# Scale maxima, masks, loads, stores and order changed in a fused attention and mixture-of-experts kernel

## The chip, the cores and the metric

The kernel runs on one core of a Trainium2 chip. Its engines work from lists of their own: TensorE (PE; PEld is its loading of weights), VectorE (DVE), ScalarE (ACT), GpSimd (POOL), and SyncE (SP), which here issues the transfers. The metric is the device time of one execution in microseconds (us), lower is better.

## The reference, cut to what matters

```python
scores = scale * np.matmul(q, k.transpose(0, 1, 3, 2))      # q, k, v: (4, 8, 576, 64)
rel = pos[:, None] - pos[None, :]
scores = np.where((rel >= 0) & (rel < 64), scores, -1000000000.0)
attn = np.exp(scores - np.max(scores, axis=-1, keepdims=True))
attn = attn / (np.sum(attn, axis=-1, keepdims=True) + 1e-09)
x = np.matmul(attn, v)                      # then reshaped to (2304, 512)

h = x @ w_in                                # 512 -> 2048
g = h * np.tanh(np.log1p(np.exp(h)))        # for h > 20: h * tanh(h)
x2 = g @ w_out                              # 2048 -> 512

logits = x2 @ phi                           # 32 slots
d = softmax(logits, axis=0); c = softmax(logits, axis=1)
slot_input = d.T @ x2                       # 8 experts with 4 slots each
slot_out[e] = np.maximum(slot_input[e] @ w1[e], 0.0) @ w2[e]
out = c @ slot_out                          # (2304, 512)
```

## The kernel before, in words

The 2304 tokens are 18 tiles of 128. Three stages run into each other.

Attention: a tile has two blocks of 64 queries, and each block sees 128 keys, its own 64 and the 64 before. `t_qk` puts the mask (a bf16 matrix of 0 and a large negative number, `cb`) into PSUM by four matmuls (L361) and adds the scores to it (L370). VectorE takes the maximum of each row (`t_max`, L379), ScalarE or VectorE turns it into a bias (`t_neg`, L384, L386), and ScalarE makes the exponentials from PSUM (`t_exp`, L392), for tile 0 with their sums, which VectorE forms for the others (`t_sum`, L398). GpSimd normalizes (`t_norm`, L406), TensorE transposes (`a_tr`, L427), ScalarE copies back (`t_trev`, L432), TensorE multiplies with the values (`t_pv`, px, L440), and ScalarE or VectorE copies x (`t_x`, L448). Since the two blocks of a tile overlap in their keys, keys come in 12 and values in 18 loads of 512 KB, with each value in two of them.

First feed-forward: h = x @ w_in. Every float32 operand is split into a high and a low half-precision part (`xh` L619, `xl` L622; `wh` L503, L505, `wl`), scaled by powers of two, and three products of the parts are summed (`u_mm`, L629: 864 matmuls of 512 columns, called H here). The scales come from bounds on the maxima: TensorE multiplies the top halves of values (`v_gram`) and of w_in (`w_abs`) with themselves (`g_gram`, L416), and VectorE takes the largest entry of the diagonal. The large matrices arrive as 64-bit words and are decoded by ScalarE (L312) and two VectorE passes (L317, L321). ScalarE applies the activation (u, L635), with a table load where the function changes. g is split again: first half on GpSimd (`u_gh`, L649) or VectorE (L653), second on VectorE (`u_gl`, L656). It is transposed by transfers. g @ w_out is not computed for the tokens: logits are g @ (w_out @ phi), and A (L817) sums the rows of g weighted with the exponentials of the logits, over ten blocks of up to two tiles, by steps lr, lt (L762), e, et (L795), A.

Tail: w_out is applied to A, then the experts (`eh` L951, relu, `ho` L967 which moves the relu's output to the rows, `eo` L982), repetition of the outputs (`or`, L996), products with the combine weights (`fo`, L1022), copies (`ob`, L1026) and stores (L1035, L1037). The combine weights are a softmax over the 32 logits of a token (`c_max` to `c_mul`), transposed (`ct`, L1067) into a buffer.

The order is made by a planner (`Plan`) at build time. It holds every step with its engine, an assumed cost, a due time and what it needs, and pools of buffers: 53 slabs of 4 KB a partition, 8 PSUM banks, and limits on some kinds. It runs through time, and on each free engine emits the ready step with the least due time; `PRM` is the table of numbers behind the due times. Where TensorE has nothing ready in the front and in the tail it emits pads (`fill`, L230), products of zeros. `reserve` keeps slabs from the early loading of the experts' 64 weight parts of 512 KB.

## Time and profile before

| | us |
|---|---|
| median of three runs | 396.62 (395.6 to 396.87) |
| the profiled execution | 396.48 |
| its span | 394.70 |

| engine | busy us | share of the span | instructions |
|---|---|---|---|
| PE | 373.4 | 95% | 4359 |
| PEld | 219.2 | 56% | 4359 |
| DVE | 250.3 | 63% | 542 |
| ACT | 257.8 | 65% | 479 |
| POOL | 84.0 | 21% | 71 |

Transfers moved 102.72 MB. Along the chain of waits that ended last, PE holds 52% of the span, ACT 20%, DVE 8%, DMA 8% and issue 7%. A share of busy time is a mean over stages: the stretches have to be looked at one by one. Pads count as busy. A record on DVE or ACT may reach into the next one, so the time that an instruction adds to a full list is a little less than its record.

### The profile page before, as it was taken

How to read it: one execution, taken by the hardware profiler on the slowest of the kernel's cores; microseconds unless marked ns; L12 is line 12 of the kernel's file. 1: busy time of each engine (PE TensorE's matmuls, PEld its weight loads, DVE VectorE, ACT ScalarE, POOL GpSimd, SP SyncE). 2: the span in 40 equal slices, each digit the busy share in tenths (PEclk: the TensorE clock that was granted, in tenths of full speed). 3: DMA queues.
4: the chain of work that ended last, by engine and by line, in shares of the span. 5: the costliest groups of instructions: out<-in, count | busy, mean ns of one | idle time of the engine just before them, and what ended most of it. 6: DMA issues, size and time to landing. Idle time of an engine off the chain costs nothing.

```text
span 394.7 us, 10510 instructions
## 1 busy us (share of the span) xinstructions
PE 373.4 (95%) x4359; PEld 219.2 (56%) x4359; DVE 250.3 (63%) x542; ACT 257.8 (65%) x479; POOL 84.0 (21%) x71
## 2 busy tenths in 40 slices
PE   7999999999999999998999998999999999999870
PEld 6686766655566655754555444454444476437750
DVE  3689899979979994779785556433332677010350
ACT  4589988999999996685889999455271361000140
POOL 0054522042864524014131212212200000000000
PEclk9999999999999999999999999999999999999995
DMA  7999997606999937778899989999999679999387
GB/s 290 406 409 392 410 406 284 215 2 152 235 272 307 302 125 173 109 96 228 160 252 282 240 227 218 236 263 273 304 270 277 133 213 390 409 408 408 152 274 207
DMA packets 103071, 102.72 MB, mean 260 GB/s; under 512 B 78704, under 2 KB 83696, under 8 KB 103024
## 3 DMA queue, kind: packets, MB, share of 16 engines
q1 hardware_dynamic: 103024, 102.06, 87.6%
q8 instruction: 34, 0.56, 0.6%
q14 instruction: 13, 0.11, 0.1%
HBM read 79.50 MB, written 4.72 MB: 213 GB/s over the span
## 4 chain that ended last, share of the span: by engine, by line
PE 52%; ACT 20%; DVE 8%; DMA 8%; issue 7%; POOL 2%; SPq 0%; DVEq 0%; POOLq 0%; ACTq 0%
PE h L629 23%; ACT L635 4%; PE eo L982 4%; DMA gT<-gg 4%; ACT p L392 4%; PE eh L951 4%; ACT u L635 3%; PE pad L230 3%; ACT L312 3%; DMA v<-in_vL 2%; PE px L440 2%; PE pt L427 2%; PE A L817 2%; PE fo L1022 2%; DMA wir<-in_w_in 2%
## 5 line engine op out<-in xcount | busy, mean ns | idle before, releaser
L629 PE MATMUL h<-wh,xx 128*128 128x512 f16 x576 | 182.5, 379 | 0.0
L629 PEld LDWEIGHTS <-xx 128*128 128x128 f16 x864 | 80.7, 97 | 89.1 <-issue 2.3
L629 PE MATMUL h<-wl,xx 128*128 128x512 f16 x288 | 109.1, 379 | 0.0
L635 ACT ACTIVATE u<-h,sc 128x512 f32<-128x512 f32 x72 | 48.1, 686 | 49.5 <-PE h L629 46.8
L406 POOL TENSOR_TENSOR p<-p,st 128x512 f32<-128x512 f32 x36 | 44.7, 1260 | 91.9 <-DVE st L402 39.7
L656 DVE SCALAR_TENSOR_TENSOR gg<-u,sc,gg 128x1024 f16<-128x1024 f32 (+1 forms) x38 | 47.5, 1253 | 25.3 <-POOL gg L649 25.1
L649 POOL TENSOR_SCALAR gg<-u,sc 128x1024 f16<-128x1024 f32 x30 | 38.4, 1285 | 110.3 <-ACT u L635 104.7
L635 ACT ACT_TABLE_LOAD x35 | 44.9, 1283 | 0.7
L392 ACT ACTIVATE p<-s,st 128x128 f32<-128x128 f32 x144 | 42.6, 403 | 0.3
L398 DVE TENSOR_REDUCE st<-p 128x4 f32<-128x512 f32 x34 | 23.0, 676 | 6.6 <-ACT p L392 6.4
L379 DVE TENSOR_REDUCE st<-s 128x4 f32<-128x512 f32 x36 | 24.4, 678 | 2.5 <-PE s L370 2.5
L312 ACT ACT_TABLE_LOAD x19 | 24.4, 1283 | 1.3 <-PEq L1204 0.7
L432 ACT COPY pts<-pt 128x512 f32<-128x512 f32 x36 | 21.4, 611 | 5.6 <-PE pt L427 5.5
L230 PE MATMUL pad<-wphi 128*64 128x256 f16 x157 | 23.1, 294 | 0.9 <-DVE wphi L240 0.9
L427 PE MATMUL pt<-cst,p 128*128 128x128 f32 x144 | 21.5, 278 | 1.5 <-POOL p L406 1.0
L440 PE MATMUL px<-pts,v 128*64 128x64 f32 x576 | 21.5, 225 | 0.4 <-DVE x L448 0.2
L440 PEld LDWEIGHTS px<-pts,v 128*64 128x64 f32 x576 | 18.8, 138 | 5.1 <-issue 1.2
L230 PEld LDWEIGHTS <-wphi 128*64 128x64 f16 x157 | 16.9, 117 | 4.9 <-issue 2.3
L370 PE MATMUL s<-k,q 64*64 64x128 f32 x576 | 19.4, 270 | 0.1
L427 PEld LDWEIGHTS pt<-cst,p 128*128 128x128 f32 x144 | 15.9, 141 | 5.9 <-issue 2.3
L370 PEld LDWEIGHTS s<-k,q 64*64 64x64 f32 x576 | 17.1, 133 | 1.4 <-issue 0.4
L982 PE MATMUL eo<-w,tw 128*32 128x64 f32 (+2 forms) x512 | 16.6, 274 | 1.1 <-issue 1.1
(166 smaller groups left out, 471.5 us busy)
## 6 DMA issues: line engine op xcount, KB each, us to landing
w<-in_wL SPq DMA_DIRECT2D x64, 512.0 KB, 6.9
v<-in_vL SPq DMA_DIRECT2D x18, 512.0 KB, 8.5
wir<-in_w_in SPq DMA_DIRECT2D x16, 512.0 KB, 9.6
wtr<-in_w_outT SPq DMA_DIRECT2D x16, 512.0 KB, 5.7
wor<-in_w_out SPq DMA_DIRECT2D x16, 512.0 KB, 4.7
k<-in_kL SPq DMA_DIRECT2D x12, 512.0 KB, 8.3
q<-in_qL SPq DMA_DIRECT2D x9, 512.0 KB, 10.1
out<-ob SPq DMA_DIRECT2D x12, 256.0 KB, 4.0
```

Source lines behind the costliest of these rows:

```text
L230: PE.matmul(pad, lhsT=hot, rhs=hot.unsqueeze(1).to_broadcast([128, 4, 64]), start=True, stop=True)
L312: ACT.activation(y[j // 2][:, j % 2], raw[j][:, :, 1].bitcast(F32), AF.Prelu, scale=2.0 ** -112, alpha=2.0 ** 32)
L370: PE.matmul(st_[t][h][64 * c:64 * c + 64, p], lhsT=qt[t // 2][r, t % 2, p, 64 * c:64 * c + 64], rhs=kt[g // 3][r, p, 64 * (g % 3):64 * (g ...
L392: ACT.activation(pr[t][:, h, p], st_[t][h][:, p], AF.Exp, scale=0.125, bias=stat[t][:, 0, 4 * h + p:4 * h + p + 1], accum_out=(stat[t][:, ...
L406: (POOL if t < P["NRM"] else DVE).tensor_tensor(pr[t][:, h], pr[t][:, h], r, ALU.mult)
L427: PE.transpose(q[:, p], pr[t][:, h, p], ident)
L440: PE.matmul(x[64 * h:64 * h + 64, p, f], lhsT=vt[t][:, c, 64 * (2 * p + h):64 * (2 * p + h) + 64], rhs=ptS[t][:, h, p, f], start=True, sto ...
L629: PE.matmul(ph[t, m], lhsT=xh[t][:, l, kk], rhs=r[m][:, kk], start=(kk == 0 and i == 0), stop=(kk == 3 and i == 2))
L635: ACT.activation(ub[t, h][:, m % 2], ph[t, m], AF.Mish, scale=col(INVH + 4 * PART[t] + m))
L649: POOL.tensor_scalar(o, u, col(CP + PART[t]), 1.0, ALU.mult, ALU.mult)
L656: DVE.scalar_tensor_tensor(gg[t, h][:, 1, c:c + n], flat(ub[t, h], c, n), col(CP + PART[t]), gg[t, h][:, 0, c:c + n], ALU.mult, ALU.subtract,)
L982: PE.matmul(tl["o", c][32 * j:32 * j + 32], lhsT=tl["hT"][:, i, kf + k].rearrange("p j s -> p (j s)"), rhs=v[:, j, k], start=(first and k ...
```

## The change

Scores carry no mask any more (72 mask matmuls go). VectorE adds the mask in the pass that takes the maxima: a tensor_tensor_reduce of 128x128 for each head, 144 in place of 36 reduces, each followed by a read of its accumulator. It writes minus an eighth of the masked scores into p, in SBUF, and the negated maximum beside it, so the negations go. The exps read p and write it in place; for tiles 0 to 3 they also sum.

Keys and values are loaded once, in nine loads each. A tile that starts in the middle of a key pair has its keys in two pieces (two score matmuls of 64 columns instead of one of 128); the values of the older 64 keys are on the other half of the rows, so their product goes to a bank of its own (py, 16 tiles), which VectorE adds to x (`t_xa`).

The maxima of the values and of half of w_in come from ScalarE: the sum of the squares of each row (`squares`, 512 wide, two each). The other half of w_in keeps its gram matrices.

GpSimd keeps 26 of 36 normalizations and 4 of 30 first halves of g, VectorE takes the others. Three x copies go from ScalarE to VectorE, three w_hi the other way. The relu's output is transposed instead of being multiplied with a selection matrix. The combine softmax is done in two parts, 12 tiles and 6, the first of them ahead of the last H, with A's buffer for the transposed weights. Two adjacent tiles share a store: 14 stores instead of 24.

The planner gets a table `SHIFT` that moves the due time of single steps, `WORK` for the slabs kept at each count of finished tiles, and other numbers. ScalarE has 53 table loads instead of 71; pads are 227 instead of 157, 178 of them (106 before) in the front.

```diff
-    90.104), PB=(2, 4, 8), LT=15, XE=400.363, FOP=-103.09, SUMA=1, XA=12, NEGA=14, GHA=2, WHA=4, KEEP=31,
+    8), LT=16, XE=405.59, FOP=-85.317, SUMA=4, XA=9, GHA=1, WHA=7, WORK=(60, 30, 43, 15, 3, 50, 30, 3, 10, 7,
...
+    39.64), TM_M=(4.58, 14.52, 15.44, 43.95), SHIFT=dict(at=(-182.55, -25.0, 4.25, 8.64, 25.3, 30.35, 28.63,
...
-            for c in range(2):
-                for h in range(2):
-                    r = slice(64 * h, 64 * h + 64)
-                    PE.matmul(
-                        st_[t][h][64 * c:64 * c + 64], lhsT=cb[r, 0, r], rhs=cb[r, 1 + ((2 * t + c) % 9 == 0)].unsqueeze(1).to_broadcast([64, 4, 128]),
...
+                        for x, k in keys(t, c, r, p):
+                            PE.matmul(
+                                st_[t][h][64 * c:64 * c + 64, p, x], lhsT=qt[t // 2][r, t % 2, p, 64 * c:64 * c + 64],
+                                rhs=k, start=True, stop=True, tile_position=(64 * h, 64 * c),
+                            )
...
-            DVE.tensor_reduce(stat[t][:, 0, 4 * h:4 * h + 4], st_[t][h], AX.X, ALU.max)
-
-        def t_neg(t, h):
...
+            m = (t % 9 == 0) + 2 * (t % 9 == 4)
+            for p in range(4):
+                DVE.tensor_tensor_reduce(
+                    out=pr[t][:, h, p], in0=st_[t][h][:, p], in1=cb[:, m], scale=-0.125, scalar=3e38, op0=ALU.add, op1=ALU.min,
+                    accum_out=stat[t][:, 0, 4 * h + p:4 * h + p + 1],
+                )
...
-                    pr[t][:, h, p], st_[t][h][:, p], AF.Exp, scale=0.125, bias=stat[t][:, 0, 4 * h + p:4 * h + p + 1],
+                    pr[t][:, h, p], pr[t][:, h, p], AF.Exp, scale=-1.0, bias=stat[t][:, 0, 4 * h + p:4 * h + p + 1],
...
+        def squares(c, x, nm):
+            o = bank(nm, [128, 512])
+            for k in range(2):
+                ACT.activation(o, x[:, k], AF.Square, accum_out=col(c + k))
...
+            parts = [(x[:, 0], 0, slice(0, 64), own), (x[:, 1], 1, slice(0, 128), own)]
+            if 2 * t % 9:
+                y = pys[t] = bank(f"py{t}", [128, 4, 64])
+                parts.insert(1, (y, 0, slice(64, 128), vt[(t - 1) // 2][:, (t - 1) % 2]))
+            for o, c, r, v in parts:
...
+                            o[64 * h:64 * h + 64, p], lhsT=v[r, 64 * (2 * p + h):64 * (2 * p + h) + 64], rhs=ptS[t][r, h, p, 64 * c:64 * c + 64],
+                            start=True, stop=True, tile_position=(r.start, 64 * h),
...
+        def t_xa(t):
+            o = xs[t // 2][:, t % 2, :, 0:64]
+            DVE.tensor_tensor(o, o, pys[t], ALU.add)
...
-                PE.matmul(o[:, k], lhsT=tl["hs"][:, c, 128 * k:128 * k + 128], rhs=cst[:, C_DG:C_DG + 32], start=True, stop=True)
+                PE.transpose(o[:, k], tl["hs"][:, c, 128 * k:128 * k + 128], ident)
...
+        CG = [(0, 12), (12, NT)]
...
+            op(f"c_tr{g}", "PE", 0.33, f, lambda g=g: c_tr(g), [f"c_mul{g}"], get=[(f"ct{g}", "b")])
+            op(f"c_ev{g}", "DVE", 0.5, f, lambda g=g: c_ev(g), [f"c_tr{g}", "tat0", "tat1"], rel=[f"ct{g}"])
```

Two places of the order. The first is TensorE in the attention. Before, around the px group of a tile in the front (the number behind a name is its buffer; xx is the split x, v the values):

```order
L629 LDWEIGHTS xx_790
L629 MATMUL h_0_994<-wl_294,xx_790 128x512
L629 LDWEIGHTS xx_790
L629 MATMUL h_0_994<-wh_283,xx_790 128x512
L262 MATMUL sb_w_1210<-cst,sc 1x128
L440 MATMUL px_1214<-pts_1149,v_842 64x64 x16
L416 LDWEIGHTS v_1124
L416 MATMUL gram_v_1234<-v_1124 128x128
```

Now, the end of the scores of an even tile and the px group behind them:

```order
L430 MATMUL s_1_497<-k_418,q_375 64x64
L430 MATMUL s_1_497<-k_267,q_375 64x64
L430 MATMUL s_0_496<-k_418,q_375 64x128
L430 MATMUL s_1_497<-k_418,q_375 64x128
L508 MATMUL px_528<-pts_461,v_178 64x64 x8
L508 MATMUL py_529<-pts_461,v_178 64x64 x8
L508 MATMUL px_528<-pts_461,v_178 64x64 x8
L326 MATMUL sb_v_474<-sc,ones 128x1
```

The gram product of the values is gone from behind px; eight py products stand between the two halves of a px group, and the scores of this tile come in pieces of 64 and 128 columns.

The second is ScalarE in the front. Before, a stretch with two tiles' exps (p from the scores s, st the statistics, wiy a decode of w_in, pts the transposed p):

```order
L392 ACTIVATE p_423<-s_0_316,st_412 128x128 x4
L432 COPY pts_385<-pt_1_418 128x512
L384 ACTIVATE st_412<-st_412 128x4
L312 ACTIVATE wiy_452<-wir_360 128x512
L392 ACTIVATE p_423<-s_1_317,st_412 128x128 x4
L448 COPY x_486<-px_454 128x512
L432 COPY pts_497<-pt_0_481 128x512
L384 ACTIVATE st_438<-st_438 128x4
L432 COPY pts_497<-pt_1_491 128x512
L392 ACTIVATE p_527<-s_0_390,st_438 128x128 x4
```

Now, a stretch with the same work (vj and wj are the squares of values and of w_in, u the activation):

```order
L575 ACTIVATE wh_928<-wi_337,sc 128x1024
L368 ACTIVATE wiy_916<-wir_456 128x512
L477 ACTIVATE vj_965,sc<-v_826 128x512 x2
L496 COPY pts_980<-pt_0_923 128x512
L448 ACTIVATE p_905<-p_905,st_904 128x128 x4
L477 ACTIVATE wj_1005,sc<-wi_648 128x512 x2
L496 COPY pts_980<-pt_1_949 128x512
L448 ACTIVATE p_905<-p_905,st_904 128x128 x4
L709 ACT_TABLE_LOAD
L709 ACTIVATE u_0_1030<-h_0_635,sc 128x512
L709 ACTIVATE u_0_644<-h_1_1018,sc 128x512
```

The negations ahead of the exps are gone, the exps read p, and squares and w_hi stand between them.

## Rows read from the trace of the kernel before

**Rows 1.** Windows: us, then busy us (count) of PE, PEld, DVE, ACT, POOL; clock, DMA share, GB/s

```profile
0.00:186.40 186.40, 180.59 (x2247) 116.29 (x2247) 157.00 (x354) 156.53 (x335) 64.31 (x54) 1.00 0.83 252
30.00:135.00 105.00, 103.58 (x1283) 66.02 (x1273) 96.49 (x205) 100.24 (x217) 42.19 (x33) 1.00 0.85 267
318.60:382.50 63.90, 62.40 (x1105) 38.99 (x1102) 22.89 (x69) 12.87 (x35) 0.00 (x0) 1.00 0.88 333
```

**Rows 2.** Chain that ended last: start us, us, what

```profile
96.86 1.14 ACT p L392 x4
...
295.30 20.73 PE h L629 x96
...
352.10 1.01 PE ho L967 x8
...
369.44 1.05 issue
```

**Rows 3.** ACT groups: line, operation, shapes, count | busy us, mean ns | idle before

```profile
L635 ACT ACT_TABLE_LOAD x35 | 44.9, 1283 | 0.7
...
L392 ACT ACTIVATE p<-s,st 128x128 f32<-128x128 f32 x144 | 42.6, 403 | 0.3
...
L432 ACT COPY pts<-pt 128x512 f32<-128x512 f32 x36 | 21.4, 611 | 5.6 <-PE pt L427 5.5
...
L312 ACT ACTIVATE wiy<-wir 128x512 f32<-128x512 f32 x16 | 11.0, 695 | 5.0 <-DMA wir<-in_w_in 4.9
...
L384 ACT ACTIVATE st<-st 128x4 f32<-128x4 f32 x28 | 6.6, 242 | 5.6 <-DVE st L379 5.6
...
L392 ACT ACTIVATION_READ_ACCUMULATOR p<-s,st 128x1 f32 x8 | 1.6, 202 | 0.0
```

**Rows 4.** Window, pads alone on PE

```profile
0.00:50.00 50.00, 16.07 (x106) 1.00 0.98 381
```

**Rows 5.** PE timeline, 134 to 144 us: start us, us, line, shapes, count [idle before]

```profile
134.32 1.15 PE L440 MATMUL px<-pts,v 128*64 128x64 f32 x32 [0.21 <-DVE x L448]
135.82 0.66 PE L427 MATMUL pt<-cst,p 128*128 128x128 f32 x4 [0.34 <-POOL p L406]
136.31 0.38 PE L629 MATMUL h<-wh,xx 128*128 128x512 f16 x1
...
140.09 0.41 PE L361 MATMUL s<-cb 64*64 64x512 bf16 x4
140.33 1.04 PE L370 MATMUL s<-k,q 64*64 64x128 f32 x32
141.31 0.39 PE L629 MATMUL h<-wh,xx 128*128 128x512 f16 x1
...
142.71 1.15 PE L440 MATMUL px<-pts,v 128*64 128x64 f32 x32
143.79 0.41 PE L416 MATMUL gram_v<-v 128*128 128x128 bf16 x4
```

**Rows 6.** PE timeline, behind 186 us

```profile
186.65 0.41 PE L762 MATMUL lt<-cst,e 128*128 128x128 f32 x2 [1.04 <-DVE e L753]
```

**Rows 7.** PE timeline, tail

```profile
372.06 1.17 PE L1022 MATMUL fo<-os,cT 32*128 32x128 f32 x32
```

**Rows 8.** DVE groups, columns as in rows 3

```profile
L656 DVE SCALAR_TENSOR_TENSOR gg<-u,sc,gg 128x1024 f16<-128x1024 f32 x34 | 44.6, 1312 | 25.3 <-POOL gg L649 25.1
...
L379 DVE TENSOR_REDUCE st<-s 128x4 f32<-128x512 f32 x36 | 24.4, 678 | 2.5 <-PE s L370 2.5
...
L321 DVE SCALAR_TENSOR_TENSOR wi<-wir,wi 128x512 uint32<-128x512 uint32 x16 | 12.6, 795 | 0.1
...
L653 DVE TENSOR_SCALAR gg<-u,sc 128x1024 f16<-128x1024 f32 x4 | 3.0, 750 | 10.6 <-ACT u L635 7.6 <-PE h L629 3.1
...
L527 DVE TENSOR_REDUCE sc<-gram_v 128x1 f32<-128x128 f32 x4 | 1.1, 286 | 0.3 <-PE gram_v L416 0.3
...
L596 DVE SCALAR_TENSOR_TENSOR wphi<-wpt,sc,wphi 128x128 f16<-128x128 f32 x4 | 1.1, 344 | 0.5 <-ACT wphi L591 0.5
```

More of the change, by code (lines that the diff above doesn't have):

```diff
@@ new lines, with group @@
+FAMILY = {x: f for f, xs in dict(
+    at="qk max exp sum rcp nrm atr tre pv x xa", xx="xh xl", mi="mi gh gl", lg="lg", b="lr l lt bm bw bexp et eh el A Aup", bz="bz brat",
+    gt="tr", wid="wia wib wid", wtd="wta wtb wtd", wod="woa wob wod", wild="wild", wtld="wtld", wold="wold",
+    k="k", q="q", v="v", vg="vg", vmm="vmm", wh="wh", wl="wl", wpmm="wpmm", wim="wim", c="c_max c_sub c_exp c_sum c_add c_rcp c_mul c_tr c_ev",
+).items() for x in xs.split()}
+def group(name):
+    f, i, rest = re.match(r"([A-Za-z_]+)(\d*)(.*)", name).groups()
+    if f == "mm":
+        return "mm", 4 * int(i) + int(rest[1])
+    return (FAMILY[f], int(i)) if f in FAMILY and i else None
@@ L56, in __init__ @@
         self.reserve = lambda: 0
+        self.tiles = 0
         self.warm = []
@@ L125, in emit @@
         n = len(self.ops)
+        prio = []
+        for o in self.ops:
+            f, i = group(o[0]) or ("", 0)
+            s = PRM["SHIFT"].get(f, ())
+            prio.append(o[3] + (s[i] if i < len(s) else 0.0))
         todo = [len(o[5]) for o in self.ops]
@@ L181, in emit @@
                 self.done.add(o[0])
+                self.tiles += o[0].startswith("mm") and o[0].endswith("_3b")
                 self.order.append((t, end, eng, o[0]))
@@ L250, in body, with place @@
         ENDS = (*[b - 1 for b in PB], NT - 1)
+        def place(t):
+            return t if t >= 16 else 4 * (t % 8 // 2) + 2 * (t // 8) + t % 2
+        scales = iter(range(9))
         def col(k):
@@ L463, in body @@
-            op(f"v{t}", "SP", 1.37, P["VP"][t] if t < len(P["VP"]) else k - P["LEAD"] + 6, lambda t=t: ld_v(t), get=[(f"v{t}", "s!"), (f"V{t}", "vv")])
-            for c in [1, 0] if 2 * t % 9 == 8 else [1]:
-                one, end = t in (0, *PB) and c == 1, t in ENDS
-                op(f"vg{t}_{c}", "PE", 0.29, k - P["LEAD"] + 6, lambda a_=(t, c, one, end): v_gram(*a_), [f"v{t}"] + ([] if one and c else [f"vg{t}_1" if not c else f"vg{t - 1}_{int((2 * t - 2) % 9 != 8)}"]),
-                   get=[(f"gram_v{PART[t]}", "b")] if one else [], rel=[f"v{t}"])
@@ L1005, in out_units @@
         def out_units(c):
-            n = min(NQ, 512 // W2C[c][1])
-            return [range(a, min(a + n, NQ)) for a in range(0, NQ, n)]
+            n, full = min(NQ, 512 // W2C[c][1]), NT // 4
+            return [range(a, min(a + n, full)) for a in range(0, full, n)] + [range(full, NQ)] * (NQ > full)
         def out_rows(c, b, i):
@@ L1183, in layouts @@
     allow = [ok, ok & (kk >= 64)]
-    masks = np.concatenate([np.where(np.eye(128) > 0, 0x3F80, 0)] + [np.where(m, 0, 0xCFEE) for m in allow], 1).astype(np.uint16)
+    keys = np.where(np.arange(128)[:, None] < 64, (kk + 64) % 128, kk)
+    masks = [np.where(np.take_along_axis(np.where(np.arange(128)[:, None] // 64 == f, allow[1], ok), keys, 1), 0, 0xCFEE) for f in (2, 0, 1)]
+    masks = np.concatenate(masks, 1).astype(np.uint16)
     for r in range(128):
```

334 lines of the change are left out of this document (179 added, 155 removed), and 4 rows, old and new, of the table VP.

## The prediction

> **What bounds the kernel now.** I read the table of windows first [rows 1]. From 30 to 135 us ScalarE is busy 100.24 of 105.00 us and VectorE 96.49, while TensorE's 103.58 there include pads and the attention's small products: whatever ends in this front, ends on ScalarE's and VectorE's lists. From 318.60 to 382.50 TensorE alone is full. The chain of waits says the same [rows 2]: four exps of 1.14 us stand in it at 96.86, a run of 96 H products at 295.30 (20.73 us, .216 each), the transposition of the relu's output at 352.10. The profiled execution took 396.48 us (394.70 of span and 1.78 around it); the median of the three runs shown is 396.62. The sum is made against 396.48. I split it at the end of the fourteenth px group, at 135.4 in before [rows 5], because there the list of ScalarE ends to decide and TensorE's stream begins to.
>
> **A, the front up to 135.4.** ScalarE's list ahead of the 28th pts copy changes so. Table loads 22 to 14: 8 x 1.283 = -10.3 [rows 3]. Four exps of .403 take 1.14, so a record overlaps the next by about .12, which I take off each of the others. Negations 28 to 0: 28 x (.242 - .12) = -3.4. Squares: 22 of them (14 of values, 8 of w_in), each 512 wide with a sum behind it; neither is in the trace. A 512-wide activation is .695 (decode, L312) and the read of a sum .202 (L392), so one costs .575 + .08 = .66, or 14.5 in all. Its bounds are .49 (the 512-wide pts copy from L432, .611, with no read) and .90 (both records whole): 10.8 to 19.7. Sums of exps 8 to 32: 24 x .08 = +2.0 (they save VectorE six reduces). One tile's eight exps come later: 8 x .285 = -2.3; three x copies fewer, at L432's price: -1.5; five wty decodes fewer: -2.9; one u fewer: -.6; three 1024-wide w_hi more, at twice the decode's .575: +3.4. Sum: -1.1. Of ScalarE's idle time 4.9 us is put down to the loads of w_in [rows 3]; 12 loads of 512 KB go (keys 12 to 9, values 18 to 9), so these land earlier: -2, between 0 and -4.9. TensorE's own list of the front: px as before, 12 py groups of 8 at .54 (half of the px group's 1.08 [rows 5]) +6.5, 12 H -2.6, 68 gram_v in fours at .24 (their record, .41, is that of four masks, which take .24) -4.1, half of w_in's gram matrices about -2, sixteen tiles' masks at .24 -3.8, one tile's scores less -1, 72 more pads at .15 [rows 4] +10.9: +3.9 in all. The pads are there to fill waits that stand in the order anyway; where ScalarE is as late as now they cost nothing, and if it were early they would cost their price. The change adds one wait here: an exp now stands behind four pairs (1.04 at .26, below) where it stood behind a reduce and a negation (.60 and .24); the .2 more is hidden while pts copies, decodes and squares stand between on ScalarE. So the front can't gain all of its 3.1: I take **-1.5**, between -5 and +4.
>
> **B, TensorE behind it.** Twelve H products come later: 12 x .216 = +2.6. One tile's scores more, two tiles' masks fewer: .98 - 2 x .24 = +.5. Twelve gram_v of values fewer, three fours of .24: -.7. Four tiles' py, each 8 products of 64x64 on the other half of the rows, issued between the two halves of px: no row shows such a pair. From above it is half of a px group, .54 each; from below 0, if they run beside px. I take .54, since px itself is issued as pairs on two column halves and its 1.08 for 32 records already holds that: +2.2. The two ho groups [rows 2] become transpositions; four of these take .49 [rows 5], eight .98, against 2 x 1.01: -1.0. Sum **+3.6**. The H products need no cover here, since TensorE is full.
>
> A px group of 32 records takes 1.08 us [rows 5], .034 a record. [...]
>
> **C, the softmax steps of the blocks.** Behind 180 TensorE has three idles ahead of the steps lt and et, of 1.04, .57 and .58; [rows 6] shows the first. The new order puts twelve H products (2.6 us) between most of these steps where six stood (1.3 us), so a lateness of at most 1.04 is covered: -2, between 0 and -2.2. What is late next is VectorE itself, and that is rival one.
>
> **D, the tail.** The first output product starts at 372.06 [rows 7], behind the second part of the transposed combine weights (ct, L1067). Its other input, the repeated columns (or, L996), is issued ahead of the 1.05 us that TensorE stands on issue from 369.44 [rows 2]. Twelve of 18 tiles' weights are now transposed ahead of the last H products and the rest earlier in the tail. The stores follow the output products to the end of the span, so what starts earlier ends earlier. They are 14 instead of 24, of up to twice the size, with rows of the same width; I give nothing for their number. If the products start where that gap begins, 2.6 is won, and the gap may go too: between 0 and -3.7, and I take -2.5. One more load of the last experts' weights goes behind the last transposition of g; it costs nothing where the loads of that stretch arrive ahead of a full TensorE [rows 1].
>
> **Sum:** -1.5 + 3.6 - 2 - 2.5 = -2.4, from 396.48: **394.1**.
>
> **VectorE's list** decides whether this holds, so its sum is needed too. Up to the second half of the eleventh tile's x (x_lo, L622) before works 157.0 of the first 186.4 us and idles 29.4 [rows 1]. In the new order TensorE asks for that tile after 252 more H products behind the fourteenth px group (54.5 us), three score groups (2.9), eight transposition groups (3.9), four px and four py groups (6.5), and 268 logits, fold and sum matmuls of few columns (an estimate of 12, at .045): at about 135.4 + 80 = 215. Ahead of it VectorE gets, less .08 of overlap each [rows 8]: maxima, 36 reduces of .60 out, 144 pairs in (a tensor_tensor_reduce of 128 elements with its read of the sum). No row shows that pair: the 128-wide reduce from PSUM is .286, so .206 from below, with a read that hides; the 128-wide scalar_tensor_tensor .344, and with a read of .1 .364 from above. I take .26, nearer the reduce, which reads one large operand from PSUM as this does: +15.8 (+8.1 to +30.8). Then 14 first halves of g at .67 +9.4; 4 more second halves at 1.23 +4.9; ten normalizations at a reduce's .60 +6.0; 16 half-wide additions of py at .35 +5.6; four x copies at .60 +2.4; eight decodes at .72 and an estimated .35 for the first pass +8.6; three w_hi fewer at .67 -2.0; six sums -3.6; eight negations about -1. Together +46 at .26, +38 to +61 at the bounds. 157.0 + 46 = 203 of 215: 12 us of idle are left where 29 were. It just fits.
>
> **Rivals.** *One, slower: VectorE becomes the bound.* The place is the products of tiles 10 to 11, at 200 to 216. At the upper price of the pair its list is 157 + 61 = 218, and with half of the old idle 233: late by 3 to 18. At .26 and all the old idle kept it would be 232. For it: VectorE is already 92% busy from 30 to 135. Against it: 25.1 us of VectorE's idle time over the whole span is waiting on GpSimd's first halves [rows 8], and these go to VectorE. It decides once more than 12 us of idle stay at .26 a pair, or more than 6 at .30. Price about +8 on the forecast: 402, chance .24.
>
> *Two, slower: exps from SBUF.* The exps now read p in SBUF and not the scores in PSUM. The bounds are 0 and the difference of 512-wide rows, .695 (SBUF) to .611 (PSUM) [rows 3], .084 x 112 = 9.4; halfway is +4.7, which falls on ScalarE's list of the front: 399, chance .10.
> [...]
>
> *Three, faster: the front really opens.* py runs beside px (-8 over 16 tiles, of which 2.2 behind 135.4), w_in lands 4.9 earlier, and the pads are the only thing between. The front then gives -5 and B gives +1.4: 394.1 - 3.5 - 2.2 = 388.4. For it: the DMA wait of 4.9 is there, and 12 of 39 loads of queries, keys and values go. Against: ScalarE's list is hardly shorter. Chance .21.
>
> The forecast itself has .45; its own range is 389.5 to 399, by A's and D's ends. This kernel's measurement can tell .3% from no change, 395.4 to 397.8 here. Of the forecast's .45 some .31 lies below 395.4, .08 between, .06 above. With the rivals: faster .31 + .21 = .52; same .08 + .03 (a mild rival two) = .11; slower .06 + .24 + .07 = .37. The range for 8 in 10 is 386.5 to 404.
>
> **What would show it.** In the new profile: the fourteenth px group ending between 131 and 137; a pair on VectorE near .26; a py group adding about half a px group; idles ahead of lt and et under .3 us; the first output product at 368 to 371 and the end 22 us behind it. It is wrong if VectorE shows no idle up to 215 and TensorE waits for x_hi or x_lo of tile 10, if the exps' records grow from .403, or if ScalarE's squares take over .9 each.

## The result, and the profile after

The changed kernel took 399.2 us in the median (397.49 to 400.43, 14 runs), the kernel before 396.44 on the same chips (395.06 to 399.75, 14 runs): a ratio of 1.0062, 95% interval 1.0039 to 1.0086. It is slower by 0.6%. The forecast of faster was wrong in its sign; the time lies inside the range for 8 in 10 (386.5 to 404) and just above the forecast's own (389.5 to 399). The profiled execution of after took 397.98, of which 396.0 is span, against a span of 394.7 before. So of the 2.8 us between the medians the two traces show 1.3; what follows accounts for these, and the rest is no part of it.

| place (us) | before | after | difference in the step |
|---|---|---|---|
| end of the fourteenth px group | 135.3 | 136.2 | +0.9 |
| last H product starts | 319.55 | 321.35 | +0.9 |
| first slot product (si) | 335.02 | 339.20 | +2.4 |
| end of the span | 394.7 | 396.0 | -2.9 |

The ends of px groups, here and below, have the .2 us by which the last record reaches into the next product taken off. One execution of each kernel is traced. e8 below runs the same instructions as after up to this place, and its fourteenth px group ends at 136.8; in the five kernels below that begin like before it ends between 135.05 and 136.2. Differences of about half a microsecond in a step are within that.

First the windows of after, with [rows 1]'s columns; the second row is a stretch that is not among those.

```profile
0.00:186.40 186.40, 180.15 (x2394) 119.96 (x2395) 158.50 (x595) 160.44 (x367) 36.28 (x34) 1.00 0.71 237
20.00:88.00 68.00, 66.63 (x962) 46.30 (x960) 60.12 (x265) 67.57 (x175) 19.76 (x18) 1.00 0.62 239
30.00:135.00 105.00, 103.20 (x1373) 67.83 (x1370) 95.14 (x351) 98.86 (x226) 31.54 (x26) 1.00 0.65 197
318.60:382.50 63.90, 62.44 (x1110) 38.22 (x1108) 23.37 (x74) 13.92 (x36) 0.74 (x1) 1.00 0.91 339
```

From 20 to 88 us ScalarE is busy 67.57 of 68.00 us; before it was 61.74 there, and TensorE 67.80. The chain of before from 12 to 88 us, the second line, lies on TensorE for 56% and on ScalarE for 25%: here it was TensorE's list that was full. ScalarE's was full behind 88 us (46.96 of 47.30 us up to 135.3), where the chain of before is 68% ScalarE and 26% VectorE.

```profile
20.00:88.00 68.00, 67.80 (x873) 45.44 (x866) 61.99 (x153) 61.74 (x138) 24.45 (x19) 1.00 0.80 306
...
by line: PE h L629 24.2%; DMA v<-in_vL 12.4%; PE pt L427 7.6%; PE px L440 7.0%; PE pad L230 6.2%; ACT p L392 5.4%; ACT L312 5.1%; PE s L370 3.4%; ACT L635 3.4%; ACT wiy L312 3.1%; ACT u L635 2.7%; ACT pts L432 2.7%; DVE st L398 2.4%; PE gra
```

In after the two stretches have changed places. Its chain from 12 to 88 us, shares by line, is 95% ScalarE (exps, squares vj and wj, decodes, copies, table loads); the one load began ahead of 12 us and is counted whole in its line.

```profile
by line: ACT p L448 34.4%; DMA wir<-in_w_in 10.8%; ACT vj L477 10.0%; ACT wiy L368 9.9%; ACT wh L575 9.6%; ACT pts L496 8.1%; ACT wj L477 7.4%; ACT L709 4.8%; ACT u L709 4.3%; ACT x L516 3.7%; issue 3.0%; ACT L448 1.7%; ACT L368 1.7%; DVE s
```

Behind 88 us the same chain lies on TensorE, 96% of it up to 136.2. These are its links where it changes over, those behind the last H product, and the one stall in the tail that stood in [rows 2] at 1.05:

```profile
86.30 1.28 ACT L709
88.43 1.21 PE pt L491 x8
...
321.73 0.23 PE lg L815 x8
321.96 0.19 PE lg L817 x8
...
336.72 0.37 PE ct L1152 x2
...
370.61 1.46 issue
```

ScalarE's groups, columns as in [rows 3]. Against the lines there, the main group of table loads has 26 for 35; new are the squares, .594 each with a read of .189, where I had used .695 and .202. The record of an exp is .391 for .403, but its group is busy for 47.9 us instead of 42.6. The wait for w_in's loads did not go: it grew from 4.9 to 9.5 us.

```profile
L709 ACT ACT_TABLE_LOAD x26 | 33.4, 1283 | 2.1 <-DVE gg L730 1.6
L448 ACT ACTIVATE p<-p,st 128x128 f32<-128x128 f32 x144 | 47.9, 391 | 2.2 <-DVE st L441 2.2
L477 ACT ACTIVATE vj<-v 128x512 f32<-128x512 f32 x18 | 10.7, 594 | 0.3
L477 ACT ACTIVATION_READ_ACCUMULATOR vj<-v 128x1 f32 x18 | 3.4, 189 | 0.0
L368 ACT ACTIVATE wiy<-wir 128x512 f32<-128x512 f32 x16 | 10.4, 672 | 9.5 <-DMA wir<-in_w_in 9.5
```

What an exp adds to the list is the time from its start to the start of what follows. Four in a row, with the instruction behind them, take 1.02 us in before (first two lines) and 1.18 in after (last two). Over all that follow each other directly the step is .249 us from PSUM and .292 from SBUF, .043 more, which is 4.8 us for the 112 exps of the front.

```profile
50.56 1.14 ACT L392 ACTIVATE p<-s,st 128x128 f32<-128x128 f32 x4
51.58 0.22 ACT L384 ACTIVATE st<-st 128x4 f32<-128x4 f32 x1
...
46.42 1.28 ACT L448 ACTIVATE p<-p,st 128x128 f32<-128x128 f32 x4
47.60 0.57 ACT L496 COPY pts<-pt 128x512 f32<-128x512 f32 x1
```

ScalarE's timeline shows where the 9.5 us stand. All are in the first 13 us, before any square or exp. They are not all lost: before, ScalarE waited 4.59 us more for the first maxima there, and its first exp started at 14.45, where it now starts at 13.40.

```profile
5.21 0.67 ACT L368 ACTIVATE wiy<-wir 128x512 f32<-128x512 f32 x1 [3.20 <-DMA wir<-in_w_in]
9.68 0.66 ACT L368 ACTIVATE wiy<-wir 128x512 f32<-128x512 f32 x1 [3.80 <-DMA wir<-in_w_in]
12.82 0.68 ACT L368 ACTIVATE wiy<-wir 128x512 f32<-128x512 f32 x1 [2.48 <-DMA wir<-in_w_in]
```

VectorE's pair of product and read, from its timeline: one starts .21 us behind the last, less than the .26 I took. Below the "..." stands the group of the second halves of g: its 25.1 us of waiting on GpSimd [rows 8] are gone.

```profile
25.83 0.28 DVE L441 CUSTOM_DVE_ANT_0 p<-s,cb 128x128 f32<-128x128 f32 x1
26.04 0.08 DVE L441 DVE_READ_ACCUMULATOR2_ANT st<- 128x1 f32 x1
26.04 0.28 DVE L441 CUSTOM_DVE_ANT_0 p<-s,cb 128x128 f32<-128x128 f32 x1
...
L730 DVE SCALAR_TENSOR_TENSOR gg<-u,sc,gg 128x1024 f16<-128x1024 f32 x34 | 44.1, 1304 | 0.4
```

TensorE's fourteenth px group, to be laid beside [rows 5], and below it the first output product, [rows 7]'s line. With py between its halves the group runs from 134.79 to 136.39 (136.2 in the table), 1.60 us by the records where px alone had 1.15:

```profile
134.79 0.51 PE L508 MATMUL px<-pts,v 64*64 64x64 f32 x10
135.26 0.51 PE L508 MATMUL py<-pts,v 64*64 64x64 f32 x11
135.70 0.69 PE L508 MATMUL px<-pts,v 128*64 128x64 f32 x16
...
374.05 1.15 PE L1095 MATMUL fo<-os,A 32*128 32x256 f32 x16
```

The pads of 20 to 90 us alone, before and then after. [rows 4] had those up to 50.

```profile
20.00:90.00 70.00, 5.06 (x36) 1.00 0.77 297
```

```profile
20.00:90.00 70.00, 11.96 (x90) 1.00 0.60 233
```

Summed by tile up to the first slot product, each product counted until the next one starts, pads take TensorE 30.51 us for 21.45, py 8.62 for none, px 18.27 for 20.43, scores and masks 18.75 for 23.17, the gram products of values none for 5.32.

### The profile page after: what moved, and what is told of

It reads as the page before. It is cut to its first block, busy times and chain, and to the rows that moved or that the text cites. A ratio compares the mean times of both kernels' runs of the same rounds, so it can differ in the third digit from the quotient of the medians.

```text
span 396.0 us, 11309 instructions
## 1 busy us (share of the span) xinstructions
PE 377.2 (95%) x4637; PEld 225.2 (57%) x4637; DVE 275.9 (70%) x839; ACT 254.1 (64%) x511; POOL 37.0 (9%) x35
## 4 chain that ended last, share of the span: by engine, by line
PE 64%; ACT 24%; DMA 4%; issue 2%; DVE 1%; SPq 1%; DVEq 0%
PE h L703 35%; ACT p L448 9%; PE eo L1055 4%; PE eh L1023 4%; PE A L892 3%; PE px L508 3%; PE pt L491 2%; ACT vj L477 2%; PE lg L815 2%; DMA wir<-in_w_in 2%; DMA gT<-gg 2%; PE fo L1095 2%; ACT wiy L368 2%; ACT wh L575 2%; PE lg L817 2%
## 5 line engine op out<-in xcount | busy, mean ns | idle before, releaser
L448 ACT ACTIVATE p<-p,st 128x128 f32<-128x128 f32 x144 | 47.9, 391 | 2.2 <-DVE st L441 2.2
L462 POOL TENSOR_TENSOR p<-p,st 128x512 f32<-128x512 f32 x26 | 31.1, 1215 | 86.9 <-DVE st L458 35.5
L727 DVE TENSOR_SCALAR gg<-u,sc 128x1024 f16<-128x1024 f32 (+1 forms) x34 | 24.9, 741 | 16.3 <-ACT u L709 13.1
L441 DVE CUSTOM_DVE_ANT_0 p<-s,cb 128x128 f32<-128x128 f32 x144 | 32.5, 283 | 1.4 <-PE s L430 1.1
L280 PE MATMUL pad<-wphi 128*64 128x256 f16 x227 | 31.9, 291 | 1.0 <-DVE wphi L290 1.0
L280 PEld LDWEIGHTS <-wphi 128*64 128x64 f16 x227 | 25.0, 117 | 5.2 <-issue 2.8
L508 PE MATMUL px<-pts,v 128*64 128x64 f32 (+1 forms) x576 | 24.7, 225 | 0.0
L508 PEld LDWEIGHTS px<-pts,v 128*64 128x64 f32 (+1 forms) x576 | 20.3, 136 | 5.6 <-issue 2.9
L430 PE MATMUL s<-k,q 64*64 64x128 f32 (+1 forms) x720 | 20.6, 256 | 2.8 <-DMA k<-in_kL 2.8
L454 DVE TENSOR_REDUCE st<-p 128x4 f32<-128x512 f32 x28 | 18.9, 677 | 6.3 <-ACT p L448 6.2
```

The costliest lines, as they stand in the source:

```text
L280: PE.matmul(pad, lhsT=hot, rhs=hot.unsqueeze(1).to_broadcast([128, 4, 64]), start=True, stop=True)
L430: PE.matmul(st_[t][h][64 * c:64 * c + 64, p, x], lhsT=qt[t // 2][r, t % 2, p, 64 * c:64 * c + 64], rhs=k, start=True, stop=True, tile_posi ...
L441: DVE.tensor_tensor_reduce(out=pr[t][:, h, p], in0=st_[t][h][:, p], in1=cb[:, m], scale=-0.125, scalar=3e38, op0=ALU.add, op1=ALU.min, acc ...
L448: ACT.activation(pr[t][:, h, p], pr[t][:, h, p], AF.Exp, scale=-1.0, bias=stat[t][:, 0, 4 * h + p:4 * h + p + 1], accum_out=(stat[t][:, 1, ...
L462: (POOL if t < P["NRM"] else DVE).tensor_tensor(pr[t][:, h], pr[t][:, h], r, ALU.mult)
L508: PE.matmul(o[64 * h:64 * h + 64, p], lhsT=v[r, 64 * (2 * p + h):64 * (2 * p + h) + 64], rhs=ptS[t][r, h, p, 64 * c:64 * c + 64], start=Tr ...
```

## The experiments

All ratios are to the kernel before, with 95% intervals; after itself has 1.0062 (1.0039 to 1.0086). The first theory was: ScalarE's list, filled up by squares, sets the front. Against it stood pads (theory 2), VectorE (rival one) and py on TensorE.

**Which list sets the front: squares, pads, VectorE, py**

e1, pads behind the first 48 of that kind not issued:

```
+            if k == 1 and made[k] > 48:
+                return 0.11
```

> The changed kernel, every engine's order as it is, but of its 227 pads the 88 that run after 20 us in the front are not issued. Theory 1 (ScalarE's list holds the front up to about 88 us, and pads fill waits that are there): the ratio to before stays at 1.006, within 0.003, and idle time of TensorE takes the place of the pads. Theory 2 (pads are time of TensorE's own list): 88 x 0.11 = 9.7 us less, ratio about 0.982. A fall of the granted clock where pads are missing would show as a slower run than the changed kernel, ratio above 1.01.

Measured 1.0067 (1.0044 to 1.009), where theory 1 had it: without these pads the kernel is no faster. Their place was not left empty for free, though. TensorE is busy 59.95 us of the 68 where it had 66.63, and in ten of them its granted clock is .74. The fourteenth px group ends at 138.7, 2.5 us later than in after, and the tail is 1.6 shorter. What the pads gave back and what the lower clock took can't be told apart here.

```profile
20.00:88.00 68.00, 59.95 (x879) 39.04 (x877) 58.43 (x261) 66.02 (x178) 19.65 (x18) 0.95 0.63 241
50.00:60.00 10.00, 5.99 (x36) 2.87 (x35) 8.89 (x28) 9.94 (x24) 3.30 (x3) 0.74 0.82 324
```

e2, squares over 64 of 512 columns:

```
-                ACT.activation(o, x[:, k], AF.Square, accum_out=col(c + k))
+                ACT.activation(o[:, 0:64], x[:, k, 0:64], AF.Square, accum_out=col(c + k))
```

> The changed kernel, order as it is, but ScalarE squares 64 columns and not 512 in each of its 26 squares (the scale maxima then come from an eighth of the values and of half of w_in). Each should be about 0.24 us shorter, by the difference of the 512-wide squares (0.594) and the 128-wide exps (0.391): 26 x 0.24 = 6.2 off ScalarE's list, 5.3 of it in the front. Theory 1: 3 to 5 us faster than the changed kernel, ratio 0.994 to 0.999. Theory 2 (TensorE's list with its pads is the bound): 0 to 1 us, ratio 1.003 to 1.007.

Measured 0.9991 (0.9966 to 1.0017), the upper end of theory 1's range. The fourteenth px group ends at 134.0, 2.2 us earlier. The chain from 12 to 88 us, nearly all on ScalarE in after, is now all on TensorE, pads included:

```profile
by line: PE h L703 32.4%; PE pad L280 21.4%; PE s L430 14.6%; PE pt L491 11.7%; PE px L508 10.2%; PE gram_w L472 3.0%; PE py L508 2.9%; PE sb_w L326 1.6%; PE sb_v L326 1.3%; PE sb_w L320 0.6%; PE sb_v L320 0.6%; issue 0.0%
```

The 22 squares ahead of that place take .22 instead of .594, 8.2 us off ScalarE, and 2.2 come through. So ScalarE's list does set the front of after, and TensorE's lies about two microseconds under it.

e3, 30 first halves of g moved from VectorE back to GpSimd:

```
+            if eng == "POOL" or (eng == "DVE" and n == 1024):
```

> The changed kernel, order as it is, but the 30 first halves of g that VectorE forms (0.776 us each) are formed by GpSimd (1.27 each): 20 us off VectorE's list, 30 us on GpSimd's. The rival that VectorE bounds the kernel: at least 3 us faster than the changed kernel, ratio below 0.999. Theories 1 and 2: VectorE has idle time to give, so no gain; GpSimd's longer time per half makes g and its transposition later, 0 to 2 us slower, ratio 1.006 to 1.012.

Measured 1.0088 (1.0059 to 1.0117): a lighter VectorE gains nothing. VectorE waits for GpSimd's halves again here, 27.7 us in all, so this run alone is not a clean test of rival one. The profile of after settles it: VectorE has 30.1 us of idle up to 215 us (184.9 busy), and 1% of the chain that ended last.

e4, py and its additions left out, so that the older keys' values are missing in the outputs:

```
+            for o, c, r, v in parts[:1] + parts[-1:]:
```

> The changed kernel, order as it is, without the 128 py products and without the 16 additions of py to x (the older 64 keys' values are then left out of the first block of each tile): 8.6 us off TensorE's list, 5.4 off VectorE's. Theory 1: what stands behind 88 us counts, some 10 of 16 tiles, 5 us, and px's first half becomes a little dearer where it no longer has py beside it, about 1: 3 to 5 us faster than the changed kernel, ratio 0.994 to 0.999. Theory 2: the whole 7 to 8.6 us, ratio 0.985 to 0.989. If neither TensorE nor VectorE were the bound: no change.

Measured 1.0045 (1.0022 to 1.0068): neither theory's range, but the third case, no change. TensorE loses 8.62 us of py, but by the same sums px's own time rises by 3.94 to 22.21 and idle time by 2.44; the fourteenth px group ends at 136.2 as in after, and the first slot product starts at 339.5 for 339.2.

e7 joins e2 and e4, e11 joins e2 and e1.

> The changed kernel, order as it is, with both the squares cut to 64 columns and the py products and their additions left out (scale maxima from an eighth of the data, older 64 keys' values missing in the first block of each tile). Short squares alone gave 0.9991, no py alone 1.0045, the changed kernel 1.0062. If ScalarE's list is the only one that binds up to the last tiles, py stays free: 0.996 to 0.999. If TensorE's list binds as soon as ScalarE's is shorter: py counts now with 3 to 6 us, ratio 0.983 to 0.991.

Measured 0.9923 (0.9896 to 0.995), between the two ranges. Alone the two edits gave .0071 and .0017, together .0139, and the trace has it at the same place: the fourteenth px group ends at 132.8, 1.2 us before e2's, while e4 alone moved it by nothing. The clock from 20 to 88 us is 1.00 in e2 and in e4, and thirty H products in a row take 6.58 us there in e7, .219 each where [rows 2] has .216. So py has a price only where ScalarE is early.

> The changed kernel, order as it is, with the squares cut to 64 columns (scale maxima from an eighth of the data) and the 88 pads behind 20 us left out. Short squares alone gave 0.9991, fewer pads alone 1.0067. If ScalarE's list and TensorE's list with its pads end nearly together, pads count as soon as ScalarE's list is shorter: ratio 0.988 to 0.995. If pads only fill waits whatever ScalarE does: 0.997 to 1.001.

Measured 0.9945 (0.9923 to 0.9966), inside the first range: .0117 together, where the squares gave .0071 and the pads nothing. By the times the pads too have a price where ScalarE is early. The traces don't show where: the px group ends at 134.0 in e2 and e11, and the spans are 392.1 and 391.8 (e2's traced execution took 394.14, its median is 396.0). The clock falls in e11 too:

```profile
50.00:60.00 10.00, 7.08 (x24) 2.94 (x23) 8.89 (x24) 9.91 (x25) 2.49 (x2) 0.66 0.81 320
```

**The other way round: load on TensorE, relief for ScalarE**

e5 replaces all squares by gram products at the same places:

```
+                    PE.matmul(o[:, k], lhsT=z, rhs=z, start=j == 0, stop=j == 3)
+            DVE.tensor_reduce(sc[:, c:c + 2], o, AX.X, ALU.max)
```

> The changed kernel with the planner's order kept, but the 26 squares (and reads of their sums) of ScalarE are replaced, at the same places of the order, by gram products on TensorE (eight matmuls of 128 columns for each load) and one reduce on VectorE for each load. 26 x 0.66 = 17 us off ScalarE's list, 6 us onto TensorE's, about 5 onto VectorE's. Theory 1 (ScalarE's list holds the front, and what it holds up is paid to the end): 4 to 8 us faster than the changed kernel, ratio 0.986 to 0.996. The rival (TensorE or VectorE holds it): 3 to 6 us slower than the changed kernel, ratio 1.013 to 1.022.

Measured 1.0325 (1.0291 to 1.0358), slower than even the rival had it. ScalarE falls to 51.85 us of the 68, the fourteenth px group ends at 144.0, and the chain up to 60 us lies on TensorE with the pads at its head:

```profile
by line: PE pad L280 24.9%; PE s L430 16.0%; DMA k<-in_kL 14.9%; PE h L707 9.6%; PE pt L495 9.4%; PE px L512 7.4%; PE gram_w L472 4.5%; PE vj L480 3.8%; PE py L512 2.3%; SPq L360 2.1%; PE sb_v L326 1.0%; PE sb_w L326 1.0%; issue 0.9%; SPq L
```

e12 is e5 with e1's pads away:

> The changed kernel with gram products in the place of all squares (1.0325 alone) and without the 88 pads behind 20 us. With the grams the chain of waits of the first 60 us lies on TensorE, a quarter of it on pads. If TensorE's list is what the grams made too long: 88 x 0.11 = 9.7 us less, ratio 1.005 to 1.012. If the grams hold TensorE up by waiting for loads or banks at their places, pads or not: ratio 1.025 to 1.033.

Measured 1.0147 (1.0124 to 1.017), between the two ranges: without the same 88 pads, whose loss gained nothing in after, the kernel is 7 us faster here. By the two traces 2.5 us of that stand at the fourteenth px group (141.5 for 144.0) and 3.9 at the first slot product. The other 2.9 lie in the tail, where no pad was taken away; e5 has a stall of TensorE there of 2.59 us, e12 one of 1.35.

e14 makes only w_in's maxima by grams, with e1's pads away:

> The changed kernel, outputs whole, order as it is: the 8 squares of w_in on ScalarE become gram products on TensorE at the same places (5.3 us off ScalarE's list, 2 onto TensorE's, 1.7 onto VectorE's), and the 88 pads behind 20 us are left out (9.7 off TensorE's). If the front ends with the later of the two lists, both are shorter now: 2 to 4 us faster than the changed kernel, ratio 0.996 to 1.001. If fewer pads bring nothing and the grams cost as in the version with all of them: 1.008 to 1.016.

Measured 1.0157 (1.012 to 1.0195), the upper end of the second case: fewer pads bring nothing, and the grams cost. The fourteenth px group ends at 140.95, 4.75 us later than in after. The clock is .83 from 50 to 60 us and .51 in ten of the tail's, where the same engine is full. The traced execution took 406.09 where the median is 402.74, so its tail is not the usual one:

```profile
50.00:60.00 10.00, 6.00 (x42) 3.56 (x43) 7.72 (x25) 9.95 (x22) 3.31 (x3) 0.83 0.81 320
380.00:390.00 10.00, 10.00 (x197) 7.54 (x198) 3.38 (x10) 3.00 (x7) 0.00 (x0) 0.51 0.49 155
```

e15 leaves out every second one of the 88 pads (`and made[k] % 2`), e16 puts seven w_hi decodes of ScalarE on GpSimd:

```
-                ACT.activation(wh[m][:, 2 * h:2 * h + 2], stg[q], AF.Copy, scale=col(SW + m))
+                POOL.tensor_scalar(wh[m][:, 2 * h:2 * h + 2], stg[q], col(SW + m), 1.0, ALU.mult, ALU.mult)
```

> The changed kernel, order as it is, without every second of the 88 pads behind 20 us (44 left out, 4.8 us). Leaving out all 88 gave 1.0067, but its profile shows the granted clock at 0.74 of full speed from 50 to 60 us, where TensorE was busy 6 of 10 us, so what the pads cost and what they keep up could not be told apart. If the clock holds at 1.00 and pads only fill waits of ScalarE's list: ratio 1.004 to 1.008. If they are time: 0.994 to 0.998.

Measured 1.0164 (1.0131 to 1.0197), far from both ranges. In the front the clock holds with half the pads, and the fourteenth px group ends at 136.8, where e8 has it with all of them. So in after a part of the pads does nothing but fill waits. The time is lost later: about 3 us from 136 to 200, where TensorE's idle time up to the last H product is 3.6 us for 1.1, and 2.4 in the tail, with a stall of 2.47 and a clock of .92 and .91 in the tens from 370 and 380. Why, stays open.

```profile
20.00:88.00 68.00, 62.95 (x920) 42.10 (x919) 60.08 (x266) 67.57 (x177) 20.10 (x18) 1.00 0.62 241
```

> The changed kernel, outputs whole, order and pads as they are: the seven w_hi of 1.15 us that ScalarE forms in the front are formed by GpSimd, which is busy 37 of 396 us. 7.2 us off ScalarE's list, nothing added to TensorE's or VectorE's. If ScalarE's list holds the front (short squares took 6.2 us off it and gained 0.7%): 2 to 4 us faster than the changed kernel, ratio 0.996 to 1.001. If the gain of the short squares came from something else: 1.004 to 1.010.

Measured 1.0034 (1.0008 to 1.0059), between the two ranges. ScalarE is down to 61.80 of 68, what it had before the change, and the fourteenth px group does not come earlier (136.9): TensorE is up at 67.27, and the chain from 12 to 88 us is 56% TensorE, 25% VectorE and 18% ScalarE. The interval overlaps after's, so no gain is shown.

```profile
20.00:88.00 68.00, 67.27 (x978) 47.29 (x976) 62.73 (x266) 61.80 (x171) 28.88 (x26) 1.00 0.63 243
```

**The tail by itself**

e8, after with each paired store split into two:

```
+            for i in range(2):
+                SP.dma_start(o[:, i:2 * len(g) - 1 + i:2], ob[b, c, h][:, :, i])
```

> The changed kernel, order as it is, but each of its 14 stores is issued as two, one for each tile (28 stores of half the size, same widths of rows). If the number of stores is worth nothing, as I predicted: ratio 1.004 to 1.008. If issuing on SyncE sets the end of the span: the 14 more stores at a few tenths of a us each, 2 to 4 us slower than the changed kernel, ratio 1.011 to 1.016.

Measured 1.012 (1.0096 to 1.0144), .6% over after, so pairing is worth something, where I had given nothing. SyncE's timeline, after and then e8, shows the stores:

```profile
375.96 16.94 SPq L1108 DMA_DIRECT2D out<-ob  x14
```

```profile
377.04 19.82 SPq L1109 DMA_DIRECT2D out<-ob  x28
```

e6 grafts after's tail, whole, into before:

> The kernel before with the new tail alone: the relu's output transposed, the combine softmax in two parts with the first ahead of the last H products, the transposed weights in A's buffer, two tiles to a store. The profiles show the stretch from the first slot product to the end at 59.7 us before and 56.8 after. If that is the tail's own worth: 2 to 3 us faster than before, ratio 0.992 to 0.995. The rival (the loads of the experts' weights or the stores set the end whatever the tail does): 0, ratio 0.998 to 1.002.

Measured 1.0018 (0.9999 to 1.0038). From the first slot product to the end it takes 57.6 us for 59.7 (after has 56.8); but the last H product to the first slot product takes 17.5 for 15.5, with 62 pads for 51. The tail's gain is paid ahead of it, and the time is the rival's.

e10 is e6 with the planner's end time raised (`XE=402.231`), so that the order up to the tail stays as it was. e13 adds to that a wait of the output products on the last load of weights, e18 the same wait from the third store on.

> The whole new tail in the kernel before, as in the earlier graft (1.0018), with the planner's end time put later by the same 1.87 us, so that the last blocks stand as before (46 pads behind the last H product where the earlier graft had 62, and before 51). In the earlier graft the stretch from the last H to the first slot product took 17.5 us where before took 15.5, and the stretch behind it 57.6 where before took 59.7. If the first is the order's doing: 1.5 to 3 us faster than before, ratio 0.992 to 0.996. If the split softmax holds up the last block's steps on VectorE in any order: ratio 0.999 to 1.002.

> The new tail in the kernel before with the last blocks' order kept, as in the graft that took 1.0085, but the output products wait until the last load of the experts' weights is issued. In that graft one load of 512 KB stood behind eleven stores on SyncE (issued at 384.7 instead of about 361), and the products that need it ended the span; its first output product ran at 368.5 where before has 372.1. If the queue order is what made it slow, and the earlier start is worth what the stores then gain: 1.5 to 4 us faster than before, ratio 0.990 to 0.996. If the tail has no worth of its own: 0.998 to 1.002.

> The new tail in the kernel before, last blocks' order kept. Only the first block of output products may run before the last load of the experts' weights is issued, so that two stores stand ahead of that load in SyncE's queue where 1.0085 had eleven, and the first output product needn't wait for all loads as in the graft that took 1.0052. First output product near 368.5 (before 372.1), the load issued near 371, its products by 377. If the tail is worth what the changed kernel's profile showed: 1 to 3 us faster than before, ratio 0.992 to 0.998. If the stores set the end at their own pace whatever starts them: 0.998 to 1.003.

Measured: 1.0085 (1.0057 to 1.0114), 1.0052 (1.0031 to 1.0072) and 1.0038 (1.002 to 1.0057), by these medians all three slower than every range given for them. From the last H product to the first slot product each takes about 15.15 us (before 15.47), so the split softmax does not hold that stretch up. In e10 the first output product starts at 368.5, 3.6 us before that of [rows 7], and the end is late, since SyncE issues the load of the last weights behind eleven stores:

```profile
370.39 14.20 SPq L1041 DMA_DIRECT2D out<-ob  x11
384.69 0.96 SPq L891 DMA_DIRECT2D w<-in_wL  x1
393.91 1.77 SPq L1041 DMA_DIRECT2D out<-ob  x3
```

In e13 the output products wait for that load and start at 374.7. In e18 the load goes behind two stores and takes 6.36 us to land, with TensorE waiting and its clock at .50 from 375 to 380. The chain's link:

```profile
370.87 6.36 DMA w<-in_wL
```

e9 is before with paired stores and the relu transposition alone, and the planner's end time as in e10:

```
+            t = 16 if g[0] == NT // 4 else 8 * h + 2 * g[0]
+            o = a["out"][128 * t:128 * t + 256 * len(g), f:f + d].rearrange("(x p) d -> p x d", p=128)
+            SP.dma_start(o, ob[b, c, h].rearrange("p n i d -> p (n i) d"))
```

> The kernel before with TensorE's order kept up to the first slot product (the end time that the planner works back from is put later by the 1.87 us that the new tail's assumed costs are longer, which alone had reordered the last blocks in the earlier graft): only the relu's output is transposed and two tiles share a store; the combine softmax stays whole. Splitting the stores of the changed kernel cost 0.6% (1.0120 against 1.0062), so pairing should be worth 2.3 us and the transposition 0.85: ratio 0.992 to 0.995. If the gain of pairing needs the earlier combine weights too: 0.997 to 1.000.

Measured 0.9983 (0.9965 to 1.0001): the best kernel here that computes everything, yet its interval holds 1. From the first slot product to the end it takes 58.5 us for 59.7, although the stall there is 1.98 for 1.05.

e17 is e9 with four w_hi on GpSimd:

> The kernel before with paired stores and the relu's output transposed (0.9983), and its four w_hi of ScalarE on GpSimd: 4.2 us off ScalarE's list of the front. If ScalarE's list holds the front of before as it does after: ratio 0.992 to 0.997. If VectorE or TensorE hold it there: 0.998 to 1.000.

Measured 1.0056 (1.0034 to 1.0077), slower than e9. The fourteenth px group ends at 137.9 for e9's 135.5. Before has ScalarE idle for 6 of the 68 us in that stretch as it is, so there was little for this edit to take away. What made it slower stays open.

## Why the prediction was wrong

**A failed, and made most of the miss.** I took -1.5 and the trace shows +0.9. By records up to the fourteenth px group ScalarE is busy 119.8 us for 118.4, +1.4 where I had -1.1, and idle 16.4 for 16.9, where I had two to win. In the list, "Table loads 22 to 14: 8 x 1.283 = -10.3" held exactly (15 for 23 in the cut), the negations are gone, and the squares step at .53 with a read of .09, .63 where I had .66. What the sum left out is the price of reading p from SBUF, which I had put under rival two: .043 an exp, 4.8 us of ScalarE's list. A smaller slip beside it: four records have three overlaps, so .157 and not .12 comes off each, and the exps that come later save .249 each where I had .285. The idle time: "these land earlier: -2" rested on a sum over the whole line without a look at where its waits stand. They stand at the first loads, and grew there, while the first exp came only 1.05 us earlier. Waits on VectorE's maxima did fall, from 5.6 to 2.2, and waits on w_in rose by as much and more.

The second fault is in what bounds the front. I read 30 to 135 us as one stretch in which all "ends on ScalarE's and VectorE's lists". Up to 88 us it was TensorE's list that was full, pads among it, and "The pads are there to fill waits that stand in the order anyway" set TensorE's +3.9 aside, on one side of a comparison that I never made: how far ScalarE's list is ahead of TensorE's. e2, e4 and e7 together show that in after they are nearly equal in length: shorter squares bring the px group 2.2 us earlier, no py alone nothing, both 3.4. Of 8.2 us off ScalarE's squares 2.2 reach the px group, and of e16's 6 none. A saving on ScalarE alone was capped at about two microseconds in these runs, and I booked it as if nothing stood under it. That ScalarE's list holds the front of after is shown by e2; how much of the loss is the exps' 4.8 us is not, since no run changed them alone.

**B and C had about the right size.** B's -1.0 for the relu's transposition lies behind the first slot product. Between the fourteenth px group and that point I had 3.6 + 1.0 - 2 = +2.6, and TensorE takes 3.3 more (203.0 for 199.7). By tile, the H products added 2.47 (I had 2.6), py 2.17 with px .36 cheaper (2.2), scores .65 (.5), the gram products of values -.87 (-.7), idle -1.66 (-2.0). In no term of mine were w_out's product into wpo, +1.03, and the transposed combine weights, +.75, which stood behind the first slot product before. py is dearer than nothing and cheaper than half a px group: 8.62 for 16 groups less 2.16 off px is 6.5 net, .40 each; by e4, which keeps the order, it is 8.62 - 3.94 = 4.7, .29 each. The measured .29 to .40 lies between the two prices that I had, nothing if py ran beside px and .54 for half of a px group.

**A stretch that looks like a missing term is none.** From the last H product to the first slot product after takes 17.85 us for 15.47. Twice as many logits lie there, 128 matmuls for 64, and two transpositions of combine weights (.37):

```profile
319.50:335.10 15.60, 2.06 (x64) 0.44 (x2) 1.00 0.92 341
```

```profile
321.60:339.20 17.60, 4.08 (x128) 0.72 (x3) 1.00 0.99 352
```

The first row is before, the second after: lines of the logits alone, +2.0 of the +2.4. But these logits were only moved. Ahead of the last H product there are 448 for 512, and by tile they take 1.8 us less there (12.39 for 14.18); up to the first slot product all logits take 15.98 us for 16.02. So the table's +0.9 and +2.4 have to be read together, as the +3.3 above. By place, the forecast missed by 2.4 in A, by .7 from there to the first slot product, and by .6 behind it, together the 3.7 between -2.4 and +1.3.

**D was right in size and wrong in reason.** From the first slot product to the end it is -2.9, where D had -2.5 and B's relu -1.0. But the first output product did not start at 368 to 371; it started at 374.05, 2.0 later than before by the clock of the run and 2.2 earlier from the first slot product. Of these 2.2, .85 are the relu's and .79 the transposed combine weights that now stand ahead; 1.06 are products of the experts (`eo`) that run later instead. The stall that I let go stayed and grew, 1.46 for 1.05 [rows 2]. And of the gain a part is the paired stores, which I gave nothing: e8 shows .6% between 14 and 28.

**Rivals.** One (VectorE): false; the pair came at .21, and VectorE kept 30 us of idle up to 215. Two (exps from SBUF): its mechanism is there, at the half price that I gave it, 4.8 us by the steps for its 4.7. The record's mean, .391 for .403, hides it. That its 399 is next to the 399.2 measured is luck: the list took the 4.8, but a load on that list came through to the time only in part, and the other terms missed by 1.3. Three (the front opens): false for the reason under A. Two lists of nearly one length in the front were none of the three.

**The range.** "389.5 to 399, by A's and D's ends" adds both ends below, and above only A's: with D's too it is 402.

Open: 1.5 of the 2.8 us between the medians; how much of A's +0.9 is the exps; what e15 loses behind the front; and why the stall in the tail is .5 to 2.6 us from kernel to kernel. With the tail's instructions unchanged, the stretch from the first slot product to the end is 55.2 us in e1 and 60.3 in e14.

## What to carry to other kernels

Before work is taken off the engine that seems to bind, measure stretch by stretch which list is full and by how much the next is behind it, and count its fillers as work for that comparison: of two lists of nearly equal length one gives little until both are cut, and the other alone then looks innocent. Price an instruction by the time from its start to the start of the next, not by its record: here the record fell from .403 to .391 us and the step rose from .249 to .292. When one stretch of an order grows, look whether the stretch ahead of it gave the same work away before it is called a cost. And look at where on the timeline a line's idle time stands before any of it is booked as a gain.

## What the runs showed of the hardware that was not expected

- A product with a sum on VectorE, 128x128 from PSUM, with its read of the sum: records of .283 and .081, one pair each .21 us in a row.
- Exps of 128x128 that follow each other directly start .292 us apart from SBUF and .249 from PSUM, though their records are .391 and .403. By the records alone the exps from SBUF would look cheaper; by the steps each is .043 dearer.
- From 50 to 60 us TensorE was busy 5.99 of 10 us in e1, 7.08 in e11 and 6.00 in e14, and its granted clock was .74, .66 and .83. With half of the pads back it was busy 8.17 us there, and the clock was 1.00 (e15).
- The issue of one load of weights behind two stores took SyncE 2.74 us in e18; the 64 of before have a median of .38 and a longest of 1.20. The load landed 6.36 us after that issue began, no later than the median of before, 6.9.
